# Two loads moved in the order of a DMA queue: attention with pooled queries and a two-branch maxout layer

## The chip, the cores and the metric

The kernel runs on one core of a Trainium2 chip. The metric is the device time of one execution in microseconds (us). The kernel before takes 358.24 us, the median of three runs (357.92 to 360.69). One further execution was profiled; every row of the profile comes from that one.

## The reference

```python
# attention: batch 8, heads 8, seq 1152, head_dim 64, float32
q_pool = q.reshape(B, H, S // 2, 2, D).mean(axis=3)        # (the pairs of neighbouring queries are averaged)
attn   = softmax(q_pool @ k.transpose(0, 1, 3, 2) / sqrt(D))
x      = (attn @ v) -> rows (batch, pooled position), columns (head, d): 4608 x 512
# maxout layer: d_model 512, d_ff 1024
out    = maximum(x @ w1, x @ w2) @ w_out                    # 4608 x 512
```

The kernel computes `maximum(h1, h2)` as `h2 + relu(h1 - h2)`: `wd = w1 - w2` gives the branch through the relu, and `w2 @ w_out` is multiplied once, ahead of time.

## The kernel before, in words

The work is cut into 32 pairs of heads (four pairs to a batch). In this text Q11, K11 and V11 are the loads of pair 11 and so on; each is 576 KB. A pair passes through these stages:

- SyncE (SP) issues the loads of Q (line 358), K (346) and V (370) into one of three buffers each, `qraw`, `kraw`, `vraw`. In DRAM a Q load has 128 rows of 4.6 KB, a K or V load has rows of 2.3 KB.
- GpSimd (POOL) adds the neighbouring queries (`cast_q`, line 435, to `qp`), and converts K (`cast_k`, line 405, to `kbf`) and V (`cast_v`, line 445, to `vE`) to bf16. It also copies exponentials that are wanted later out of the way (`keep_rest`, line 468).
- K is transposed by a DMA that SP issues (`ktrans`, line 475, `kbf` to `kT`); Q is transposed by VectorE (DVE) in eight instructions (`qtrans_dve`, line 485, `qp` to `qpT`). The first five pairs take another way, through TensorE (PE).
- PE makes scores (line 302) in groups of 512 columns for two heads into PSUM banks `ps`; ScalarE (ACT) takes the exponential of each group (line 317) into `et`.
- PE multiplies the exponentials by V (lines 621 and 636), DVE divides by the sums (651, 654) into `xnat` and `xend`, and these are transposed to `xT`, mostly by a DMA of SP (lines 703, 712).
- The maxout layer runs in between: PE's h jobs (line 760), relu by DVE or ACT (771, 775), PE's p jobs (line 803), a copy to `stage` (809, 812), and two or more DMA stores from SP for each p job (lines 829, 835).

Nothing loops on the chip: all instructions are written out in the order of one long string, and one letter adds one operation to the program of one engine. `S` is a group of scores, `E` the exponential of the oldest group, `A` a piece of attention times V, digits are pieces of the maxout layer; `l` is the next load of a list of loads, `t` the next DMA transposition of K, `x` the next DMA transposition of the attention output, `o` the next store. Each engine runs its own operations in the order of the string and waits on semaphores for what they need. SP thus has one queue, and all its operations, a wait among them, hold up those behind:

```python
sp_line = {"l": [lambda a=a: {"q": load_q, "k": load_k, "v": load_v, "w": w_load}[a[0]](*a[1:])
                 for a in LOADS if a[-1] != "ACT"],
           "t": [lambda i=i: ktrans(i) for i in range(K_PE, NPAIR)],
           "x": [...],
           "o": [go for n in range(NP) for go in store_p(n)], ...}
```

A load also waits for ACT, so that loads do not run too far ahead. Where it stands in the string decides for which exponential: `done[0]` is the group of the last `E` ahead of it.

```python
def pace():
    g = done[0] - PACE                     # PACE = 2
    return [f"E{g}"] if PACE and g >= PACE_FROM else []
```

Of the kernel before, what the change touches and what calls it, by code (L numbers as in the profile page):

```python
# [116 lines left out]
def bass_funnel_attn__then__act_maxout2_kernel(  # L117
# [78 lines left out]
    with ctx:  # L196
# [728 lines left out]
        def step(c):  # L925
            if c == "S":
                m = int(next(banks))
                scores(group[0], m)
                exp_at.extend((group[0], go) for go in exps(group[0], m))
                group[0] += 1  # L930
            elif c == "E":
                g, go = exp_at.pop(0)
                go()
                done[0] = g
            elif c in lines or c in "0123":
                if c not in opened:
                    job = (moe if c in "0123" else lines[c]).pop(0)
                    opened[c] = job, int(next(banks)), list(job.units)
                job, m, units = opened[c]
                r, cost, mode, fence, go = units.pop(0)  # L940
                op("PE", lambda e: go(e, m), r=r, w=[f"b{m + n}" for n in range(job.width)], cost=cost,
                   mode=mode, fence=fence, tag=job.name)
                if not units:
                    del opened[c]
                    emptying.setdefault(c, []).extend((ev, job, m) for ev in job.evac)
            elif c in evacs:
                ev, job, m = emptying[evacs[c][0]].pop(0)
                eng, fn, cost = ev["eng"], ev["fn"], ev["cost"]
                if evacs[c][1]:
                    eng, (fn, cost) = "ACT", ev["alt"]  # L950
                op(eng, lambda e: fn(e, m), r=ev["r"] + [f"b{m + n}" for n in range(job.width)], w=ev["w"],
                   after=ev["after"], cost=cost, tag=("ev",) + job.name, alt=(ev["alt"] or (0, 0))[1])
            else:
                simple[c].pop(0)()
# [2 lines left out]
                 "m": ("Z", 0), "4": ("0", 0), "5": ("1", 0), "6": ("2", 0), "7": ("3", 0),  # L957
                 "8": ("0", 1), "9": ("1", 1), "+": ("2", 1), "-": ("3", 1)}
        for c in (
            "luFFlulllfyKQklgfbSkKEFlgFKSgESyFFlKEFgQSbESlFkSFEFFKlEySFSgESlqFFEFQlSbEFkSQElbKvSEgSlESceAAEATcESA"  # L960
            "EAhlkSaSEaASclEKAEglSAEcSAElvSaTaEhElTcSAESlAhAEScAElSSAcEAAlAqESa0a00aE0la0ScAE0SldQEaa00bSd0lEXSj0"
            "00ESvTl0h0E00eS4SlEAAkAEAlSa1ad1E1S1SEl1q1S1E1Kl1g1qE1S1SE1lQkrAEbArSdtAErArSE11avlEa1S5AElSdArESSrA"
            "dArEArSAEkAlaAaSEaAdatAESaXadjXEjSjSEXq0jl00jE0S0qr0E0lSr01rE11e41Sl1E1Sk1r10Er005St0ESv00r0ESSr0rvE"
            "lA4AAEASqalSaEAArAErAlSrSEEaAeaAArxAErSSaAEaAklrAAErS1at1ak1E1r0Sr0xE0r0Sr11E1rS1r0E050Sl0E0q0SrS0tE"
            "r01r10Er0eS0r0E0r0Skr0lE0r1S0r0E0rlSv0r1E14S11El1S1oSE1oAAEASAkEAaAlaSAEtAvSa1aE1SxS11ES111E1111ES11"
            "l1ESq5AAEAlSrSoEAroArAESrkSArEAaAalAEAaAaSvaaEtaSSrXEqArAjAEAjSrle00Ea0aS0rSE0lr0vSr0E1r01rlE114S11E"
            "1S1rSEA5AlvAEASr0E0ta0Eva0SrSE00xe00SE4AAkAESSlAEAaAaAEAlSa1aE1Sx000E0Sk11E0lS11E11S50qlE00tS00ESer0"
            "0rSE00rS0rE00r00Er0l0qSrSE0r01l1r0E14S11E1l1SroSE1r1o11roSErAoArAtEkArAAaaAArq1ESaa1E1Sx001r001E1r0S"
            "1rE0l001rS141E1rS1r1ES5AAEvAAroSSrvoESAlAAEvAaAaAlEAaAkaSa000SaEt0a000011114Ee111S111115E1S111Xl5EvS"
            "j00j0ESl0qSE0000SEl4AAAEArSSaEAaArAlqEArS1a1taE11rSESrE1e1xrS1r1EA5AAEASla0kaE0Sr00rSEq0l0r0SEr0ArAl"  # L970
            "E4SAAESr11aE1a1Srx1ESr11r1SEt5qAAAEArSe0aE0a0Slr0SEkr0S0r0E0lrS0r0E0r0Sl0rE0000ES0S0Er0tArAEArArS0aE"
            "0aq0Srx10Er1S14k1E1S11EroS1rSo1E1oAAoEvAAS1vElSAAlEAvAaSa1ESalAaAAEASa1aE1taS1rXvE1rS1j11Ej1eSrl11rE"
            "11qrSS5EAlAAkEAroS0a0oEa0S0rS0ErAAlAEASa0a0E0l0S4x00E0qSE0r00E0trSA4eAEAArS1a1Ea1k1Sr11ESr1lSr1E5AAA"
            "lEArS1a1Ea11Srx00E10S1l1E1S500tE0Sq0rS0Er00r0e0ESr00rSEl0kr00r0E0rS0l0ES00SE0A4AAEAAaAoaAoASaoSqaE11"
            "x11SESkr11t1rE11rE11rE1SrS1E1r11r1SEr11S1E1S11E1A5AEvAASoSvESlAAoAEvAaAaAElAaAa0Sa0a0E0taS00r0000E04"
            "e0Sx000r0E11141vS1x1E11r100500Sr11qE1Sr01lr110E1rS050E0Sl0r0E0SS0l0E0S0r0EArAArEAArlAkaAaArSE0etEa0a"
            "S0r0SE0rxS0rq0EA4AAEASkao1aE11o1SSE11lS11EA5AAElASa1aE1Sx0r00E0rS1rt0E0er0Sr0E1S4111ESl1r0q0E500S0lE"
            "0SrS0r0EA4lAAEAAAaaAASa1aESlk1Sx1r1ES1r11Ert11r11Er1qSSr1E1rArAEvAS1E11klS11El11vS1E1S1lvA5ESAAEAoAa"
            "oSaSESaAtaArAEArq00Ea0aSa00rExSv0r00ErS0xe0r0E0rSSr0kl0E0S00E0Sl00E0S00El0A4AEAAAaoSaSEoArAtArE00Ea0"
            "0aeS00rxE1111r00qS411E1111151S1k1E1r1Sl00500ESr000SrEl0A4AAEArSla1aE1S1S1EAAAEAlSa1aE1tSrS1rq1E1r1x1"  # L980
            "1rESSre11Er11rSk1Elr11S1E11Sl1E1A5AAEASaoSaEAoAAoEAoSa0a0tEq00rSESr0E00rx00k040E0AArvAArSrSvElArArAE"
            "AvaAaAAaAaSaSaE00a001x14E11S11E1x11Sv511E100S1SE0r1t11r0ES0500E0eSr00Er00SrSE0r00r0SEr0S00E0S00E0004"
            "0E00S0E0oS00oSE4AAAEAAaAaAeAAaEAaAAxAaAaAASa0aES0x00SE1000E0S411E1S11E111500S0E00S11E1S11E1S10E50S00"
            "E0S10E0Se10E00S00E0S00E0S00E10S41E11S11EoS11o1E1oSSo1E1AAEAAAaAaAAAaAaAxAAAAAaAaAAaAa1a1a1a11X1j11j1"
            "11111900001111111150000111o080110091o110000008101110191101000018111009101110000080101111191100000001"
            "001111910000000011111111110001000800110000o008001o11o00010181111Z9ZZZZZoZZoZZZZZZmZZZZzzZZZZZZZZZZmZ"
            "ZZZZZZzZzmzz"
        ):
            step(c)
# [52 lines left out]
```

## Time and profile before

| | |
|---|---|
| median of 3 runs | 358.24 us (357.92 to 360.69) |
| the profiled execution's own time | 358.12 us |
| its span, first to last instruction | 356.4 us |
| granted TensorE clock | 0.999 |
| PE busy | 346.0 us, 97% |
| ACT busy | 313.8 us, 88% |
| DVE busy | 230.1 us, 65% |
| POOL busy | 151.4 us, 42% |

Times within the profile count from the start of the span. PE is matrix multiplication, PEld the loading of its weights, which overlaps with it; both are issued in one stream. In a timeline row stand start, length, engine (a q means its sequencer: such rows are issues of DMAs, waits included), line, operation, names, shapes and how many instructions are merged; in square brackets the idle time before it and what ended it. "issue" there is idle time that nothing in the profile ended. A row of DMA issues ends with the size of one and the time from issue to landing.

### The profile page before, as it was taken

The numbers are of one execution on the slowest core, as the hardware profiler recorded it, in microseconds if no ns is written. First come the engines' busy times: TensorE is split into PE (matmuls) and PEld (weight loads), VectorE is DVE, ScalarE is ACT, GpSimd is POOL, SyncE is SP. The second block draws the span as 40 slices with busy tenths as digits, with TensorE's granted clock in tenths as the row PEclk, the third lists the DMA queues.
The fourth block names the chain that finished last, engine by engine and source line by source line (L and its number), as shares of the span: only waits on it lengthen the run. The fifth ranks groups of instructions, "written<-read, shape, count | busy, mean of one in ns | idle before, by whom it ended". The sixth has DMA issues, their size and how long they took to land.

```text
span 356.4 us, 13757 instructions
## 1 busy us (share of the span) xinstructions
PE 346.0 (97%) x6178; PEld 218.5 (61%) x6178; DVE 230.1 (65%) x472; ACT 313.8 (88%) x354; POOL 151.4 (42%) x136
## 2 busy tenths in 40 slices
PE   7889999999899999999999999999999999999996
PEld 5556665656564675656666576556576757448753
DVE  2587589974966867985887677785586875414001
ACT  5999999999999899999999989989999796992431
POOL 2625997554564264355544455227444621010000
PEclk9999999999999999999999999999999999999999
DMA  8999999999989989998999699998999943012215
GB/s 271 403 397 398 370 255 309 280 289 261 293 252 279 315 196 350 237 301 183 278 320 260 153 230 301 237 314 234 224 299 255 267 68 75 17 32 47 61 31 148
DMA packets 76699, 84.55 MB, mean 237 GB/s; under 512 B 48480, under 2 KB 49760, under 8 KB 76640
## 3 DMA queue, kind: packets, MB, share of 16 engines
q1 hardware_dynamic: 75856, 83.15, 87.5%
q8 instruction: 48, 0.79, 0.9%
q10 hardware_dynamic: 784, 0.52, 0.5%
q14 instruction: 11, 0.09, 0.1%
HBM read 62.91 MB, written 9.44 MB: 203 GB/s over the span
## 4 chain that ended last, share of the span: by engine, by line
PE 87%; ACT 9%; DMA 2%; issue 1%; SPq 0%; DVE 0%
PE ps L803 25%; PE ps L621 20%; PE ps L302 19%; PE ps L760 16%; ACT et L317 9%; PE ps L636 3%; PE ps L593 2%; DMA qraw<-in_q_dram 2%; PE ps L846 1%; PE ps L552 0%; PE ps L533 0%; SPq L346 0%; DVE qp L428 0%; SPq L358 0%; PE ps L730 0%
## 5 line engine op out<-in xcount | busy, mean ns | idle before, releaser
L317 ACT ACTIVATE et<-ps 128x1024 bf16<-128x1024 f32 (+1 forms) x336 | 302.4, 1019 | 14.5 <-PE ps L302 9.7
L302 PE MATMUL ps<-qpT,kT 64*128 64x256 bf16 (+7 forms) x1162 | 117.3, 283 | 2.7 <-issue 1.1
L485 DVE STREAM_TRANSPOSE qpT<-qp 32x288 bf16<-32x288 bf16 x216 | 101.4, 469 | 10.4 <-PE ps L302 6.1
L760 PE MATMUL ps<-xT,wd 64*128 64x512 bf16 (+3 forms) x832 | 81.2, 311 | 0.2
L302 PEld LDWEIGHTS ps<-qpT,kT 64*128 64x128 bf16 x1162 | 48.3, 94 | 49.7 <-ACT et L317 11.3
L803 PE MATMUL ps<-wo,stage 64*128 64x512 bf16 x544 | 76.4, 376 | 0.0
L435 POOL TENSOR_TENSOR qp<-qraw 128x576 bf16<-128x576 f32 x30 | 42.1, 1406 | 61.1 <-DMA qraw<-in_q_dram 57.3
L621 PEld LDWEIGHTS ps<-vE,et 128*128 128x128 bf16 x1728 | 54.9, 97 | 13.9 <-ACT et L317 9.3
L621 PE MATMUL ps<-vE,et 128*128 128x65 bf16 x1728 | 60.7, 193 | 0.7 <-issue 0.3
L771 DVE TENSOR_SCALAR stage<-ps 128x1024 bf16<-128x1024 f32 (+3 forms) x41 | 39.7, 970 | 21.1 <-PE ps L760 20.6
L760 PEld LDWEIGHTS ps<-xT,wd 64*128 64x128 bf16 x832 | 35.6, 94 | 22.2 <-PE ps L760 1.9
L405 POOL TENSOR_SCALAR kbf<-kraw 128x1152 bf16<-128x1152 f32 x31 | 35.7, 1153 | 26.3 <-DMA kraw<-in_k_dram 25.6
L803 PE MATMUL ps<-w,xT 64*128 64x512 bf16 x272 | 40.8, 377 | 0.0
L803 PEld LDWEIGHTS ps<-wo,stage 64*128 64x128 bf16 x544 | 26.4, 94 | 20.5
L445 POOL TENSOR_SCALAR vE<-vraw 128x1152 bf16<-128x1152 f32 x24 | 27.4, 1154 | 19.4 <-PE ps L636 10.8
L809 DVE COPY stage<-ps 128x1024 f32<-128x1024 f32 x14 | 17.1, 1224 | 23.1 <-PE ps L803 23.0
L468 POOL TENSOR_SCALAR stage<-et 128x1152 bf16<-128x1152 bf16 x14 | 16.1, 1152 | 35.5 <-ACT et L317 35.5
L654 DVE TENSOR_TENSOR xnat<-ps,rc 128x256 bf16<-128x256 f32 (+2 forms) x71 | 27.6, 397 | 2.0
L651 DVE RECIPROCAL rc<-ps 128x4 f32<-128x4 f32 (+2 forms) x64 | 11.6, 182 | 25.9 <-PE ps L621 25.5
L621 PEld LDWEIGHTS ps<-stage,et 128*128 128x128 bf16 x576 | 18.1, 97 | 2.7 <-issue 2.6
L621 PE MATMUL ps<-stage,et 128*128 128x65 bf16 x576 | 19.7, 193 | 0.0
L803 PEld LDWEIGHTS ps<-w,xT 64*128 64x128 bf16 x272 | 12.5, 94 | 8.8 <-DVE stage L771 0.2
(55 smaller groups left out, 155.4 us busy)
## 6 DMA issues: line engine op xcount, KB each, us to landing
vraw<-in_v_dram SPq DMA_DIRECT2D x32, 576.0 KB, 6.1
kraw<-in_k_dram SPq DMA_DIRECT2D x31, 576.0 KB, 6.7
qraw<-in_q_dram SPq DMA_DIRECT2D x31, 576.0 KB, 6.3
out_dram<-stage SPq DMA_DIRECT2D x24, 256.0 KB, 4.1
out_dram<-stage SPq DMA_DIRECT2D x21, 128.0 KB, 3.4
xT<-in_moe_w_dram SPq DMA_DIRECT2D x4, 512.0 KB, 12.2
stage<-in_moe_w_out_dram SPq DMA_DIRECT2D x4, 512.0 KB, 14.1
stage<-in_moe_w_dram SPq DMA_DIRECT2D x4, 512.0 KB, 13.2
```

What stands on the lines that cost most here:

```text
L302: last = e.matmul(ps[:, h, col:col + hi - lo], kT[i % 3][rows(h), t, :], qpT[i % 3][rows(h), lo:hi], start=True, stop=True)
L317: op("ACT", lambda e: e.activation(et2[:, :, c:c + z - a], ps[:, :, a - g * W:z - g * W], EXP, scale=scale), r=[f"b{m}", f"b{m + 1}"], w=w ...
L405: op("POOL", lambda g: g.tensor_scalar(kbf[s][:, :, :, :].rearrange("p t h d -> p h t d"), kraw[r][:, :, :, :], 1.0, 1.0, ALU.mult, ALU.mu ...
L435: op("POOL", lambda g: g.tensor_tensor(qpf[s][:, :, :], qraw[r][:, :, 0, :], qraw[r][:, :, 1, :], ALU.add), r=[f"qraw{r}"], w=[f"qp{s}.0", ...
L445: return g.tensor_scalar(vE[r][:, :, :, 0:D].rearrange("p t h d -> p h t d"), vraw[s][:, :, :, :], 1.0, 1.0, ALU.mult, ALU.mult)
L485: op("DVE", lambda e: e.transpose(view[dst:dst + 32, :, 32 * pb:32 * pb + 32], qpf[s][src:src + 32, :, 32 * db:32 * db + 32]), r=[f"qp{s}. ...
L621: last = e.matmul(fb[m][:, at * 66:at * 66 + 65], et[:, a:a + P], vE[vs][:, t, half, 0:65], start=(t == 0), stop=(t == NT - 1))
L654: todo.append(evac_op("DVE", lambda e, m, z=z, at=at, num=num, dst=dst: e.tensor_tensor(dst, a(m)[z, at:at + num, 0:D], rc[k][z, at:at + n ...
L760: last = e.matmul(fb[m + k][:, 0:size], wd[z, ct, (f0 + k) * P:(f0 + k + 1) * P], xT[z, ct, n0:n1], start=(turn == 0 and ct == 0), stop=(t ...
L771: return e.tensor_scalar_max(gT[:, f0:f0 + 2, g0:g0 + size], wide[m // 2][:, :, 0:size], 0.0)
L803: last = e.matmul(fb[m + k][:, :], lhs, rhs, start=(turn == 0 and j == 0), stop=(turn == 1 and j == NC_ + NF - 1))
L809: return e.tensor_copy(osb2[:, o:o + 2, :], wide[m // 2][:, :, :])
```

## The change

Two loads take a later place in SP's queue:

- The load of Q11 stood between the load of V8 and two stores of the output (both of one p job); it now comes behind these two stores, ahead of V9. By its place it waits for the exponential of group 85 instead of 84.
- The load of K29 stood between the load of Q29 and two stores, which are followed by the DMA transposition of K28 and one of the attention output; it now comes behind the two stores and the transposition of K28, ahead of the other transposition. By its place it waits for the exponential of group 260 instead of 258.

Nothing else in SP's order changes, the other loads wait for the same exponentials, and PE, ACT, DVE and POOL keep their orders. The string is otherwise written with other letters for the same thing: jobs of the maxout layer go by the digits 0 to 3 where they went by 0 and 1, and operations of different engines stand in another order to each other. The two places in the string (before, then after; the load is the `l` under the mark):

```diff
-            "l1ESq5AAEAlSrSoEAroArAESrkSArEAaAalAEAaAaSvaaEtaSSrXEqArAjAEAjSrle00Ea0aS0rSE0lr0vSr0E1r01rlE114S11E"
+            "333ES7AAEAkSroSEArolArAErSSrAElAavAaAEAaAaSaSaEStarXErAqAjAEljArS0ae0Ea0Sr0SElr0v0Sr0Elr10r1E114S11E"
# Q11:  before  ...AAEA l SrS o EAr o ArAE...        after  ...AkSr o SEAr o l ArAE...
-            "oSaSESaAtaArAEArq00Ea0aSa00rExSv0r00ErS0xe0r0E0rSSr0kl0E0S00E0Sl00E0S00El0A4AEAAAaoSaSEoArAtArE00Ea0"
+            "oSaSESaAtaqArAEAr22Eav2aSa22rExS2er22ErS2x2rk2E2rSSr2l2E2S22El2S22E2S22E2A6AEAAAaoSaSEoArAtlArE00Ea0"
# K29:  before  ...E l 0A4AEAAAa o SaSE o ArA t ArE...    after  ...A6AEAAAa o SaSE o ArA t l ArE...
```

More of the change, by code (lines that the diff above doesn't have):

```diff
@@ L959, in bass_funnel_attn__then__act_maxout2_kernel @@
         for c in (
[L960 to L964, printed above, removed]
@@ L965, in bass_funnel_attn__then__act_maxout2_kernel @@
-            "r01r10Er0eS0r0E0r0Skr0lE0r1S0r0E0rlSv0r1E14S11El1S1oSE1oAAEASAkEAaAlaSAEtAvSa1aE1SxS11ES111E1111ES11"
-            "l1ESq5AAEAlSrSoEAroArAESrkSArEAaAalAEAaAaSvaaEtaSSrXEqArAjAEAjSrle00Ea0aS0rSE0lr0vSr0E1r01rlE114S11E"
-            "1S1rSEA5AlvAEASr0E0ta0Eva0SrSE00xe00SE4AAkAESSlAEAaAaAEAlSa1aE1Sx000E0Sk11E0lS11E11S50qlE00tS00ESer0"
-            "0rSE00rS0rE00r00Er0l0qSrSE0r01l1r0E14S11E1l1SroSE1r1o11roSErAoArAtEkArAAaaAArq1ESaa1E1Sx001r001E1r0S"
-            "1rE0l001rS141E1rS1r1ES5AAEvAAroSSrvoESAlAAEvAaAaAlEAaAkaSa000SaEt0a000011114Ee111S111115E1S111Xl5EvS"
@@ L970, in bass_funnel_attn__then__act_maxout2_kernel @@
[L970 to L978, printed above, removed]
-            "oSaSESaAtaArAEArq00Ea0aSa00rExSv0r00ErS0xe0r0E0rSSr0kl0E0S00E0Sl00E0S00El0A4AEAAAaoSaSEoArAtArE00Ea0"
@@ L980, in bass_funnel_attn__then__act_maxout2_kernel @@
[L980 to L984, printed above, removed]
@@ L985, in bass_funnel_attn__then__act_maxout2_kernel @@
-            "11111900001111111150000111o080110091o110000008101110191101000018111009101110000080101111191100000001"
-            "001111910000000011111111110001000800110000o008001o11o00010181111Z9ZZZZZoZZoZZZZZZmZZZZzzZZZZZZZZZZmZ"
+            "lululllllyFFlflfKQglkblSkKlFEgFKlSgylESFFlKFEglQSblESlkFSlFEFFlKylSEFlSglESqlFFFElQSlbFEklSQEbKlvgES"
+            "SSElcAelAEATcESAhEAkSaSaEASlcEKAEgScAESAvESaaTEhETcSAESAhAEScAESScEqAEAaAaAaSa0E0c000dSAE0aSadQE0b0S"
+            "0vEXSj000EST0Eh0e00S4SEkAAAEAdSa1a1E1S1qSE11S1E1Kq1g1E1S1SkrE1QAEbdAtrSArEArvSlE1a1Ea1S5AdElSArESdSr"
@@ new lines, in bass_funnel_attn__then__act_maxout2_kernel @@
+            "AArEArkSAElAaAadtSEaAaAESadXajXEjSjSqElX2j22jE2qrS2r2El2Sr2e3El6333S3kE3rS3r30Evt070S0ESv0r00rESSr0E"
+            "l4qAAAElASaSaEArAArEArSSElaEAeaArAxAErSkSaaAElArAktArESa1a11Erx12rS2E2r2Sr11Er1Sr1q2El252S2E22rSSr2t"
+            "E23r32Er2eSr22Elr22Srk2E2r3Sr2v2Elr2Sr23E36S33El3S3oSE3oAkAEASAElAvaAaSAEtASa3aE3SxS33ES333E333q3ElS"
+            "333ES7AAEAkSroSEArolArAErSSrAElAavAaAEAaAaSaSaEStarXErAqAjAEljArS0ae0Ea0Sr0SElr0v0Sr0Elr10r1E114S11E"
+            "1Sr1vSEl5AAAEAvrS2aE2ta2E2erSSE22x2k2SE6AAAElSSAEAaAaAElASa3kaE3Sx000E0S33El0S3q3El33S70E0t0S00ErSe0"
@@ new lines, in bass_funnel_attn__then__act_maxout2_kernel @@
+            "r0SE0r0Sr0E0qr00r0El0r0SSrEl00r110E14S11El11SroSE1r1o11roSkErAoArAtEArAqAaaAAr1ESaa1E1Srx221r221E1r2"
+            "S1rEl22216S1r1E1Sr11ES5AAEvAAroSSrovESAlAEAlvAaAaAEAakAaSa333SaEt3a333300007Ee000S022224El2Sv222X6ES"
+            "j11qj1ElS1SE1111SEl5AAAEArSqSaElAaArAEArS3a3taE33rSESrE3e3xrS3r3EAk7AAElASa0aE0Sr00rSElq00r0SElr0ArA"
+            "E4SAAESr22aE2a2Srx2ESr22r2SEt6qAAAEArSe1aEl1a1Sr1SkEr1S1r1El1rS1r1El1r1S1rE1111ES1S1Er1tArAEArqArS1a"
+            "E1a1Srkx31Er3S353E3S33EroS3rSo3E3oAAoEvAAS3vElSAlAEAvAaSa3ElSaAaAAEASa3vaE3taS3rXE3reS3j33Elj3Srq33r"
@@ new lines, in bass_funnel_attn__then__act_maxout2_kernel @@
+            "E33rSS7kElAAAEAroS0a0oEa0S0rS0ElrAAAEASa0a0El0q2xS422E2SE2r2et2E2rSA6AEAAkrS1a1Ea11Sr11ElSr1Sr1El5AA"
+            "AEArS3a3Ea33Srx00E30S3l3E3qS700tE0S0rS0Er0e0r00ESr0k0rSEl0r00r0El0rS00ES00SE0A4AAEAAaAoqaAoASaoSaE22"
+            "kx22SESr22t2rE22rE22rE2SrS2E2r22r2SEr22S2E2S22E2A6AEvAASoSvESlAAoAEvAaAaAElAaAa1Sa1a1E1taS11r1133E35"
+            "e3Sx333r3E00070vS0x0E00r2114q11Sr22El2Sr12r221E2rS161El1S1r1El1SS11E1S1r1EArAkArEAArAaAeaArSElt1Ea1a"
+            "S1qr1xSE1rS1r1EkA5AAEASao3aE33o3SSEl33S33EA7AAElASa0aE0Sx2r22E2rS0rt2E2er2Sr2E0S6q000ElS0r11El411S1E"
@@ new lines, in bass_funnel_attn__then__act_maxout2_kernel @@
+            "1SrS1r1ElA5AAEAAAaaAkASa3aElS3xS3r3ES3r3t3Er3q3r33Er3SSr3E3rArAEvAS3E33klS33El33vS3El3S3vA7ESAAEAoAa"
+            "oSaSESaAtaqArAEAr22Eav2aSa22rExS2er22ErS2x2rk2E2rSSr2l2E2S22El2S22E2S22E2A6AEAAAaoSaSEoArAtlArE00Ea0"
+            "0aeS00rE1111rx00qS411E1133353S33El3r3S22722ESr222SrEl2A6AAElArSka0aE0S0S0EAAAElASa0aE0tSrS0r0Eq0r0x0"
+            "0rESSr0e0Er00rS0kElr00S0El00S0E0A4AAEASaoSaEAoAAoEAoSa1aq1tE11rSESr1E11rkx13353E3AArvArASrSvElArArAE"
+            "AvaAaAAaAaSaSaE33a332x27E22vS22E2x20S600E011S0SE1r0t00r1ES1411E1eSr11Er11SrSE1r11r1SEr1S11E1S11E1135"
@@ L987, in bass_funnel_attn__then__act_maxout2_kernel @@
+            "3E33S3E3oS33oSE7AAAEAAaAaAeAAaEAaAAxAaAaAASa2aES2x22SE0222E2S600E0S00E001433S3E33S11E1S11E1S13E53S33"
+            "E3S23E3Se23E33S33E3S33E3S33E23S72E22S22EoS22o2E2oSSo2E2AAEAAAaAaAAAaAaAxAAAAAaAaAAaAa2a2a2a22X2j22j2"
+            "20000+11110000333341111333o2923022-0o00222211+01000138331311123933322-0200022221+1010003383311111113"
+            "113332-21111111122222222221112100900220000o338332o22o333232-2222Z+ZZZZZoZZoZZZZZZmZZZZzzZZZZZZZZZZmZ"
             "ZZZZZZzZzmzz"
```

## The prediction

> **What bounds the kernel.** I read the page first, then the PE's timeline for the moments at which it stands still, then ACT, the queue of SyncE (SP) and the DMA packets around the two places of the change.
>
> ```profile
> span 356.4 us, 13757 instructions
> PE 346.0 (97%) x6178; PEld 218.5 (61%) x6178; DVE 230.1 (65%) x472; ACT 313.8 (88%) x354; POOL 151.4 (42%) x136
> q8 instruction: 48, 0.79, 0.9%
> PE 87%; ACT 9%; DMA 2%; issue 1%; SPq 0%; DVE 0%
> ```
>
> The chain that ended last is PE for 87% and PE is busy for 97%. A load that is issued at another moment can change the end only if PE or ACT waits less or more for it. The third line is a queue that carries instructions: 48 packets, 0.79 MB, so about 16 KB each. PE's 6178 matmuls and 6178 weight loads make 257 instructions per packet. I take this queue to be the refill of PE's instruction stream, in blocks of 256.
>
> PE has two gaps that no semaphore ends:
>
> ```profile
> 29.04 1.13 PE L621 MATMUL ps<-vE,et 128*128 128x65 bf16 x32 [0.35 <-issue]
> 92.70 0.61 PE L302 MATMUL ps<-qpT,kT 64*128 64x128 bf16 x8 [1.12 <-issue]
> 29.03:92.69 63.66, 61.99 (x1146) 38.46 (x1146) 47.31 (x101) 63.07 (x70) 43.83 (x38) 1.00 1.06 309
> 86.84:92.69 5.85, 4.73 (x140) 3.57 (x135) 5.38 (x14) 5.79 (x7) 3.29 (x4) 1.00 1.07 361
> ```
>
> The last two rows are sums over a stretch: its length, then busy time and count for PE, PEld, DVE, ACT and POOL, and at the end clock, DMA share and GB/s. Between the two gaps lie 1146 + 1146 = 2292 instructions, and 9 x 256 is 2304 (a few of PE's semaphore instructions are not in these counts). So both gaps stand at a seam between blocks: PE came to the end of a block and the next one was not there. The block before the second gap began at about 86.84 (140 + 135 instructions, with those that overlap the edges), and PE used it up in 4.73 us, because it holds many short 65-column matmuls. I take it that PE asks for the next block when it begins one, here at 86.84.
>
> Was the refill late? These are the DMA packets in four adjoining stretches (87.2 to 88.7, 88.7 to 90.25, 90.25 to 90.35, 90.35 to 91.5), and the instruction row of the third and of 26.5 to 26.6:
>
> ```profile
> DMA packets 265, 0.55 MB, mean 365 GB/s; under 512 B 29, under 2 KB 29, under 8 KB 265
> DMA packets 161, 0.63 MB, mean 406 GB/s; under 512 B 16, under 2 KB 16, under 8 KB 161
> DMA packets 31, 0.05 MB, mean 472 GB/s; under 512 B 15, under 2 KB 15, under 8 KB 30
> DMA packets 230, 0.44 MB, mean 381 GB/s; under 512 B 16, under 2 KB 16, under 8 KB 230
> q8 instruction: 1, 0.02, 68.5%
> q8 instruction: 1, 0.02, 69.3%
> ```
>
> Without the tiny packets the mean sizes are 0.55 MB / 236 = 2.3 KB (a V or K row of 9 x 64 floats), 0.63 / 145 = 4.3 KB (nearly all Q rows of 4.6 KB) and, after the refill, 0.44 / 214 = 2.05 KB (output rows of 2 KB). So the 16 engines did V8, then Q11, then PE's refill at 90.25 to 90.35, then the stores: the refill stood in line behind Q11. It took 68.5% x 16 x 0.1 = 1.10 us, so it ended near 91.4; PE went on at 92.70, 1.30 later. At the first gap the refill of 26.5 took 1.11 and PE went on 1.4 after its end. PE reached the seam at 92.70 - 1.12 = 91.58.
>
> The Trainium skill (page "Runtime: NRT & Kernel Launch", section "Instruction fetch mechanics") has the same 16 KiB blocks of 256 instructions, and calls the crossing mostly hidden. The trace agrees on the blocks; at 46 of the 48 refills it is hidden, and twice it costs 0.35 and 1.12 us.
>
> **The change, part one: Q11 behind two stores.** SP's queue around it (V8, Q11, two stores, V9), and the time from issue to landing of Q11 and of the stores:
>
> ```profile
> 84.72 0.58 SPq L370 DMA_DIRECT2D vraw<-in_v_dram  x1
> 86.13 0.34 SPq L358 DMA_DIRECT2D qraw<-in_q_dram  x1
> 87.48 1.27 SPq L829 DMA_DIRECT2D out_dram<-stage  x2
> 88.88 0.90 SPq L370 DMA_DIRECT2D vraw<-in_v_dram  x1
> qraw<-in_q_dram SPq DMA_DIRECT2D x1, 576.0 KB, 6.3
> out_dram<-stage SPq DMA_DIRECT2D x2, 256.0 KB, 4.9
> ```
>
> Now Q11 is issued at 86.13, ahead of the request of 86.84; the stores wait on SP for DVE's copy until 87.48. After the change Q11 is issued at 87.48 + 1.27 = 88.75, behind that request. By its place in the order string it also waits for the exponential one group later than before (85 for 84); groups take ACT under 1 us each, so at 88.75 that wait is long over. Nothing else on SP moves: V9 comes up behind Q11 at 89.1 (with Q11's 0.34), and now ends its issue, wait included, at 88.88 + 0.90 = 89.78.
>
> The refill then has V8 alone in front. Q11's own transfer is 576 KB at 406 GB/s = 1.45 us, so the refill starts at about 90.30 - 1.45 = 88.85, ends at 89.95, and PE could go on at 91.25, before it arrives at 91.58. The gap goes, with 0.33 us to spare. Bounds: the refill starts between 88.7 (V8's last packets) and 90.30 (no change), so the gap that is left is 0 to 1.12; I take 0.
>
> PE's 1.12 us is not all won. ACT's rows there, and the weight loads that wait for ACT next:
>
> ```profile
> 93.13 27.47 ACT L317 ACTIVATE et<-ps 128x1024 bf16<-128x1024 f32 x31 [0.49 <-PE ps L302]
> 97.07 0.76 PEld L760 LDWEIGHTS ps<-xT,wd 64*128 64x128 bf16 x10 [0.15 <-ACT et L317]
> 99.82 1.14 PEld L621 LDWEIGHTS ps<-vE,et 128*128 128x128 bf16 x36 [0.24 <-ACT et L317]
> ```
>
> ACT lost only 0.49 us to the gap: it was still at older exponentials. After it ACT runs 27.47 us with no idle time, and PE waits for ACT again from 97.07 on. PE would come there 1.12 earlier and wait longer; what moves the rest of the program is ACT's 0.49. Bounds 0.49 and 1.12; I take **0.5**, since the waits are within 5 us and the order is fixed.
>
> Late next are Q11 and its users; these are POOL's rows for Q11, a copy of exponentials and V9, and DVE's transpositions of Q11:
>
> ```profile
> 92.53 1.41 POOL L435 TENSOR_TENSOR qp<-qraw 128x576 bf16<-128x576 f32 x1 [1.80 <-DMA qraw<-in_q_dram]
> 93.90 1.16 POOL L468 TENSOR_SCALAR rem<-et 128x1152 bf16<-128x1152 bf16 x1
> 95.52 1.16 POOL L445 TENSOR_SCALAR vE<-vraw 128x1152 bf16<-128x1152 f32 x1 [0.46 <-DMA vraw<-in_v_dram]
> 95.31 2.38 DVE L485 STREAM_TRANSPOSE qpT<-qp 32x288 bf16<-32x288 bf16 x5
> ```
>
> The same bytes pass in another order. Q11 lands now at 86.13 + 6.3 = 92.4; behind the stores it lands between 93.0 (the second store, issued near 88.1, plus 4.9) and 93.8 (512 KB at 381 GB/s, 1.38 us, later); I take 93.4. POOL then adds the halves from 93.5 to 94.9, and DVE wants them at 95.31, or 94.8 after the gain. That hides it but for 0.1; with 93.8 DVE's five transpositions, and what is queued on DVE behind them, start 0.5 late, one for one. The copy of exponentials and V9 slip by 1.1 and 0.6, within POOL's idle time. The stores land up to 1.45 earlier, which nobody waits for here. Cost: 0, bounds 0 and 0.5.
>
> **Part two: K29 behind two stores and the transposition of K28.**
>
> ```profile
> 255.18 0.37 SPq L346 DMA_DIRECT2D kraw<-in_k_dram  x1
> 257.63 1.28 SPq L829 DMA_DIRECT2D out_dram<-stage  x2
> 259.01 2.53 SPq L475 DMA_TRANSPOSE kT<-kbf  x1
> 261.58 1.33 SPq L703 DMA_TRANSPOSE xT<-xnat  x1
> 262.96 0.57 SPq L370 DMA_DIRECT2D vraw<-in_v_dram  x1
> 268.77 1.68 SPq L475 DMA_TRANSPOSE kT<-kbf  x1
> kraw<-in_k_dram SPq DMA_DIRECT2D x1, 576.0 KB, 7.7
> kT<-kbf SPq DMA_TRANSPOSE x1, 6.3
> 262.96 1.15 POOL L405 TENSOR_SCALAR kbf<-kraw 128x1152 bf16<-128x1152 f32 x1 [0.89 <-DMA kraw<-in_k_dram]
> 270.35 1.40 POOL L435 TENSOR_TENSOR qp<-qraw 128x576 bf16<-128x576 f32 x1 [6.23 <-DMA qraw<-in_q_dram]
> ```
>
> K29 is issued at 259.01 + 2.53 = 261.55 instead of 255.18, 6.4 us later, and waits for exponential 260 instead of 258, which changes nothing by then. It lands behind K28's transposition, which lands now at 259.01 + 6.3 = 265.3: at the latest 265.3 + 1.45 = 266.8, at the earliest 1.45 sooner. POOL's conversion then ends by 268.0, and SP asks for it at 268.77 (transposition of K29). POOL's next work starts at 270.35. So K29 is hidden by 0.8 us; if it were later than that, the transposition and SP's queue behind it would slip one for one. The earlier landing of K28 wins nothing that a row shows as waited for. SP's next instruction, a transposition of the attention output, starts 0.4 later with K29's 0.37 ahead of it, and V29 behind that at 263.3 at the latest. The refill of PE that now has K29 ahead of it comes 1.45 sooner, but PE has no gap there to lose. Cost: 0, bounds 0 and the third rival's.
>
> **Sum.** 358.12 (the profiled execution: span 356.4 and 1.7 around it) - 0.5 = 357.6. That execution is 0.12 under the median of 358.24, so the forecast is **357.7**.
>
> **Rivals.** *The refill does not stand in line.* If PE's refill takes turns with SP's queue, Q11 does not hold it, the start at 90.30 is its own latency, and the gap stays: 358.2. For it: at most refills the gap does not come although loads are in flight. Against it: the packets lie exactly behind Q11 and ahead of the stores. The Trainium skill ("DMA: Bandwidth & Descriptors", section "Queues, rings and completion order") says just this, that each engine goes round its queues packet by packet; by that rule the time would be this rival's. The rows above speak for a line, so I give it 0.15.
>
> *The whole gap comes through.* PE keeps its 1.12 because ACT's run is itself short of work here and there: 358.24 - 1.12 = 357.1. Against it stand the waits for ACT from 97.07 on. 0.15.
>
> *Slower: a new gap at the seam near 271.* K29 now splits two transpositions and lies ahead of another refill. Rows: that refill (in the stretch 266.65 to 266.75), PE's count from the seam before it and PE at the seam after it, and the DMA share in 40 slices of 263 to 265:
>
> ```profile
> q8 instruction: 1, 0.02, 64.9%
> 263.92:271.13 7.21, 7.21 (x132) 4.63 (x128) 4.95 (x13) 7.21 (x9) 0.98 (x2) 1.00 1.06 360
> DMA  1214123922910114000089999999999999999999
> ```
>
> The refill ends at 266.70 + 64.9% x 16 x 0.1 = 267.74 and is usable at 269.04; PE is at the seam at about 271.1: 2.0 to spare. K29 ahead of it takes 1.45, and the next transposition, now alone, can add an idle stretch of its own like that of 263 to 264 (a share of a tenth or two): 1.0 to 2.0. Together 2.45 to 3.45, less what K28's transposition comes sooner (0 to 1.45). It decides from 2.0 on; the worst is a gap of 1.45, and if the first gap stays too, 359.7; with the first gain, 358.24 - 0.5 + 1.45 = 359.2. I give it 0.2 at **359.2**.
>
> **Chances.** Forecast 0.45, whole gap 0.15, no refill effect 0.15, new gap 0.2, something unseen 0.05, of either sign. The range runs from 357.1 less 0.3 (the spread of the two lower runs) = 356.8 to 359.7. One per cent, 3.6 us, is about what a measurement of this kernel can tell from no change, and no case above reaches it; only the unseen does. Faster by over 1% 0.03, within 0.91, slower 0.06.
>
> **What would show it.** Right: PE has no gap near 91 to 93 and the refill there starts by 89; ACT's idle time of 0.49 is gone; Q11's addition on POOL starts near 93.5; K29's conversion near 267; no gap at 270 to 272. Wrong: the gap near 91.6 remains with the stores ahead of the refill (no line), a gap marked issue appears near 271 (the slower rival), DVE idles before Q11's transpositions, or the transposition of K29 waits for POOL.

## The result, and the profile after

The changed kernel takes **360.01 us** (median of 22 runs, 358.53 to 363.11); the kernel before, run beside it on the same chip, 358.81 (22 runs, 356.96 to 360.69). The ratio of the runs compared is **1.0044, 95% interval 1.0029 to 1.0058**: 1.6 us slower, between 1.0 and 2.1. The forecast was 0.5 faster.

The page of the changed kernel, its span, busy times and chain, and two rows of PE's waits (total, times, longest):

```profile
span 358.0 us, 13756 instructions
PE 346.8 (97%) x6177; PEld 218.3 (61%) x6178; DVE 230.3 (64%) x472; ACT 313.8 (88%) x354; POOL 151.4 (42%) x136
PE 82%; ACT 12%; DMA 3%; DVE 1%; issue 1%; POOL 0%
PE ps L621 <- issue: 1.8, 2, 1.6
PE ps L302 <- DVE stage L771: 1.1, 1, 1.1
```

The span grew by 1.6. PE has the same instructions as before (one record is missing); its busy time is 0.8 longer, a rough figure since the ends of matmuls are modelled, and the rest is waiting. PE's timeline says where; these are the two gaps at seams that are left, the place of the old gap, and a gap at 99 that DVE ends:

```profile
28.32 1.22 PE L621 MATMUL ps<-vE,et 128*128 128x65 bf16 x35 [0.24 <-issue]
90.46 0.87 PE L302 MATMUL ps<-qpT,kT 64*128 64x64 bf16 x12
99.34 0.39 PE L302 MATMUL ps<-qpT,kT 64*128 64x64 bf16 x4 [1.13 <-DVE stage L771]
284.47 1.49 PE L621 MATMUL ps<-stage,et 128*128 128x65 bf16 x44 [1.56 <-issue]
```

The 1.12 us at 92.70 is gone: the scores at 90.46 run on, twelve in a row, where before the last eight stood and waited. In its place are 1.13 at 99.34 and 1.56 at 284.47, one behind each place of the change.

**Part one, the chain behind Q11.** SP's rows, the issue row of Q11 with its time to landing, and the packets in the stretches 87 to 88 (two rows), 88 to 89.5 (two rows), 89.5 to 90.2 and 90.2 to 91.2; the last row is of before, for the stores' stretch 90.35 to 91.5:

```profile
86.76 1.28 SPq L829 DMA_DIRECT2D out_dram<-stage  x2
88.09 1.46 SPq L358 DMA_DIRECT2D qraw<-in_q_dram  x1
89.61 0.44 SPq L370 DMA_DIRECT2D vraw<-in_v_dram  x1
qraw<-in_q_dram SPq DMA_DIRECT2D x1, 576.0 KB, 6.0
DMA packets 145, 0.31 MB, mean 311 GB/s; under 512 B 16, under 2 KB 16, under 8 KB 144
q8 instruction: 1, 0.02, 6.9%
DMA packets 146, 0.28 MB, mean 184 GB/s; under 512 B 11, under 2 KB 11, under 8 KB 146
q1 hardware_dynamic: 146, 0.28, 88.0%
DMA packets 121, 0.23 MB, mean 325 GB/s; under 512 B 10, under 2 KB 10, under 8 KB 121
DMA packets 54, 0.17 MB, mean 173 GB/s; under 512 B 11, under 2 KB 11, under 8 KB 54
q1 hardware_dynamic: 230, 0.44, 100.1%
```

The refill passes between 87 and 88, right behind V8, instead of at 90.25. But then the engines are slow. While SP waits for DVE's copy until 86.76, only V8 is under way, where before Q11 lay behind it; from 88 to 89.5 the engines move 184 GB/s (365 to 406 in the stretches before), and again 173 around the first packets of Q11. They do not stand idle for most of this: the packets of 88 to 89.5 filled 88.0% of the engines' time. Each packet took longer: 88.0% x 16 x 1.5 us / 146 = 0.145 us, where those of the stores before took 100.1% x 16 x 1.15 / 230 = 0.080. Why they do is open. Q11 lands at 88.09 + 6.0 = 94.1. To set executions beside each other I count from DVE's copy (line 809) that the stores wait for, at 85.51 here and 86.23 before: in the frame of before Q11 lands at 94.8, and there it was 92.4. It is **2.4 us later**. What that does, on POOL, DVE and ACT:

```profile
94.21 1.40 POOL L435 TENSOR_TENSOR qp<-qraw 128x576 bf16<-128x576 f32 x1 [4.51 <-DMA qraw<-in_q_dram]
95.65 2.40 DVE L485 STREAM_TRANSPOSE qpT<-qp 32x288 bf16<-32x288 bf16 x5 [1.50 <-POOL qp L435]
98.06 1.23 DVE L771 TENSOR_SCALAR stage<-ps 128x1024 bf16<-128x1024 f32 x1
99.77 1.02 ACT L317 ACTIVATE et<-ps 128x1024 bf16<-128x1024 f32 x1 [0.52 <-PE ps L302]
101.29 5.78 ACT L317 ACTIVATE et<-ps 128x256 bf16<-128x256 f32 x7 [0.49 <-PE ps L302]
```

DVE stands 1.50 before Q11's transpositions. Queued behind them is the relu of an h job at 98.06, which must empty two PSUM banks before PE can put its next scores there (99.34, 1.13 late); ACT then runs dry twice, for 0.52 and 0.49. The net of gain and loss is the time from the copy to the third relu (line 771), both released by PE; before, then after:

```profile
86.23 1.22 DVE L809 COPY stage<-ps 128x1024 f32<-128x1024 f32 x1 [3.58 <-PE ps L803]
103.62 1.22 DVE L771 TENSOR_SCALAR stage<-ps 128x1024 bf16<-128x1024 f32 x1 [1.04 <-PE ps L760]
85.51 1.23 DVE L809 COPY stage<-ps 128x1024 f32<-128x1024 f32 x1 [3.58 <-PE ps L803]
103.54 1.23 DVE L771 TENSOR_SCALAR stage<-ps 128x1024 bf16<-128x1024 f32 x1 [0.85 <-PE ps L760]
```

That is 17.39 before and 18.03 after: 0.64 longer. The copy itself comes 0.72 earlier in the changed kernel, with nothing changed ahead of it, so the two executions stand level again at the third relu. The 1.6 between the spans is therefore lost behind it.

**Part two, the chain behind K29.** K29, Q31 and K31 on SP; POOL's conversion of K29, its addition of Q31 and conversion of K31; and PE's refill in the stretch 281.6 to 281.8:

```profile
261.52 0.58 SPq L346 DMA_DIRECT2D kraw<-in_k_dram  x1
272.87 0.61 SPq L358 DMA_DIRECT2D qraw<-in_q_dram  x1
273.52 1.56 SPq L346 DMA_DIRECT2D kraw<-in_k_dram  x1
267.09 1.15 POOL L405 TENSOR_SCALAR kbf<-kraw 128x1152 bf16<-128x1152 f32 x1 [4.76 <-DMA kraw<-in_k_dram]
279.98 1.41 POOL L435 TENSOR_TENSOR qp<-qraw 128x576 bf16<-128x576 f32 x1 [4.40 <-DMA qraw<-in_q_dram]
281.56 1.15 POOL L405 TENSOR_SCALAR kbf<-kraw 128x1152 bf16<-128x1152 f32 x1 [0.17 <-DMA kraw<-in_k_dram]
q8 instruction: 1, 0.02, 38.8%
```

The same of before: Q31 and K31 on SP, on POOL, and the refill, here in the stretch 279.2 to 279.6:

```profile
271.80 0.57 SPq L358 DMA_DIRECT2D qraw<-in_q_dram  x1
272.57 0.37 SPq L346 DMA_DIRECT2D kraw<-in_k_dram  x1
277.75 1.40 POOL L435 TENSOR_TENSOR qp<-qraw 128x576 bf16<-128x576 f32 x1 [3.76 <-DVE rc L651]
279.33 1.15 POOL L405 TENSOR_SCALAR kbf<-kraw 128x1152 bf16<-128x1152 f32 x1 [0.19 <-DMA kraw<-in_k_dram]
q8 instruction: 1, 0.02, 16.5%
```

K29 itself is hidden, converted by 268.24, ahead of its transposition. But Q31 and K31 follow 1.1 and 1.0 later on SP and land some 2.2 later. PE began the block before this seam at 278.3 in both (256 instructions back from it); the refill started near 279.2 before and near 281.7 after, behind those loads. It took 38.8% x 16 x 0.2 = 1.24 us, so it ended near 282.9, and PE went on 1.5 later, at 284.47.

### The profile page after: what moved, and what is told of

The parts are those of the page before. It is cut to its first block, busy times and chain, and to the rows that moved or that the text cites. A ratio compares the mean times of both kernels' runs of the same rounds, so it can differ in the third digit from the quotient of the medians.

```text
span 358.0 us, 13756 instructions
## 1 busy us (share of the span) xinstructions
PE 346.8 (97%) x6177; PEld 218.3 (61%) x6178; DVE 230.3 (64%) x472; ACT 313.8 (88%) x354; POOL 151.4 (42%) x136
## 4 chain that ended last, share of the span: by engine, by line
PE 82%; ACT 12%; DMA 3%; DVE 1%; issue 1%; POOL 0%
PE ps L803 24%; PE ps L621 19%; PE ps L302 18%; PE ps L760 15%; ACT et L317 12%; PE ps L636 2%; PE ps L593 2%; DMA qraw<-in_q_dram 2%; PE ps L846 1%; DMA kraw<-in_k_dram 1%; DVE qpT L485 1%; PE ps L552 0%; POOL qp L435 0%; DVE stage L771 0%; PE ps L533 0%
```

## The experiments

**Theories.** For part one: the refill gain is real, but Q11 comes 2.4 late, and through DVE's fixed order (Q11's transpositions ahead of the relu) costs more than the gain. The rival: the gap at 99 is a matter of this one execution, or comes from part two. For part two, theory A: K29 between the two DMA transpositions slows the queue because it parts them. Theory B: the place among the transpositions does not matter; K29's transfer simply comes late, and what follows is pushed back. The rival to both: the gap at 283 comes and goes by chance.

Each kernel below but the changed one was run 12 times (before_fill12 10, before_fill20 13) with the kernel before beside it (358.63, 358.67 and 358.64 us in the three sets). Ratios are to that (that of after is from its own 22 runs); "copy to relu" is the time from line 809 to the third 771 as above; the gaps are PE's idle times, "issue" at 92 and 283, DVE at 99, with those under 0.13 us given as 0.

| kernel | ratio (95%) | copy to relu | gap at 92 | at 99 | at 283 |
|---|---|---|---|---|---|
| before | | 17.39 | 1.12 | 0 | 0 |
| before_again | 0.9979 (0.9950 to 1.0009) | 17.10 | 0.83 | 0 | 0 |
| k_only | 1.0006 (0.9978 to 1.0034) | 17.53 | 1.26 | 0 | 0.32 |
| k_stores | 1.0003 (0.9976 to 1.0031) | 17.08 | 0.80 | 0 | 0.83 |
| k_behind | 1.0024 (0.9999 to 1.0050) | 17.18 | 0.92 | 0 | 0 |
| after | 1.0044 (1.0029 to 1.0058) | 18.03 | 0 | 1.13 | 1.56 |
| after_again | 1.0048 (1.0017 to 1.0078) | 17.73 | 0 | 0.83 | 0.33 |
| q_only | 1.0010 (0.9980 to 1.0039) | 18.36 | 0 | 1.45 | 0.66 |
| q_dve | 1.0001 (0.9978 to 1.0025) | 16.67 | 0 | 0 | 0 |
| after_dve | 1.0021 (0.9998 to 1.0044) | 17.04 | 0 | 0.22 | 0.88 |
| v9_first | 1.0045 (1.0017 to 1.0072) | 18.05 | 1.10 | 0.44 | 0.23 |
| before_fill12 | 1.0081 (1.0051 to 1.0110) | 16.94 | 0 | 0 | 0 |
| before_fill20 | 1.0020 (0.9998 to 1.0041) | | | | |
| after_fill44 | 1.0035 (1.0012 to 1.0057) | 17.61 | 0.53 | 0 | 0.28 |

**q_only: part one alone.**

```diff
-  ESq5AAEA l SrSoEAroArAESrkS          (cut from the string, spaces set around the l)
+  ESq5AAEASrSoEAro l ArAESrkS
```

> Only Q11 goes behind the two stores; K29 stays. Theory (two costs): the PE gap near 91 to 93 is gone, but the DMA engines run half empty while the stores wait, Q11 lands over 1 us later than I forecast, DVE starts Q11's transpositions about 1.5 us late, and PE has a gap of about 1.1 us near 99 to 100 that DVE's copy at line 771 ends. Gain and loss nearly cancel: -0.5 to +0.6 us, no gap near 283. Rival (K29 is harmless, all of the loss of 1.6 us is Q11's): 1.6 us slower. Rival (my forecast; the gap near 99 is chance): 0.5 us faster, no gap near 99.

```profile
85.78 1.23 DVE L809 COPY stage<-ps 128x1024 f32<-128x1024 f32 x1 [3.58 <-PE ps L803]
104.14 1.22 DVE L771 TENSOR_SCALAR stage<-ps 128x1024 bf16<-128x1024 f32 x1 [0.85 <-PE ps L760]
99.93 0.39 PE L302 MATMUL ps<-qpT,kT 64*128 64x64 bf16 x4 [1.45 <-DVE stage L771]
284.15 1.49 PE L621 MATMUL ps<-stage,et 128*128 128x65 bf16 x44 [0.66 <-issue]
```

The gap at 99 is part one's own, with part two undone: 104.14 - 85.78 = 18.36. But there is a gap at 283 too, with K29 at its old place. That speaks for chance in part two. In time it is 359.36, a ratio that could be 0.7 us faster or 1.4 slower; the times alone do not settle part one, the profile does.

**q_dve: the same, with DVE's order changed.** Six of Q11's eight transpositions go behind relus that they stood ahead of. The cut gives DVE's order and not the string (r is a transposition, h a relu, three dots are other work):

```diff
-  r r r r r h4 r h5 r ... r h6
+  r r h4 r h5 r ... r r h6 ... r r
```

> Q11 behind the two stores, and six of its eight transpositions on DVE put behind the copies of the h jobs that they stood ahead of. Theory (Q11 costs only through DVE's order): no gap of PE near 91 to 93 and none near 99, and the gain of the forecast appears: 0.5 us faster than before, 0.5 to 1.1 faster than Q11 alone. Rival (what PE lost near 99 comes from another wait, such as the banks or the exponentials): the gap near 99 stays and the time is that of Q11 alone.

```profile
86.47 1.23 DVE L809 COPY stage<-ps 128x1024 f32<-128x1024 f32 x1 [3.58 <-PE ps L803]
103.14 1.23 DVE L771 TENSOR_SCALAR stage<-ps 128x1024 bf16<-128x1024 f32 x1 [0.54 <-PE ps L760]
```

Q11 is nearly as late as in q_only (its transpositions start 10.2 after the copy, there 10.5), but the relus no longer stand behind all of it: the gap at 99 is gone and the stretch is 16.67, shorter than before's. So the loss runs through DVE's order, and with that out of the way the refill's gain shows in this stretch. The time, 358.42, does not beat the kernel before: the 0.5 us that were expected lie inside its interval and are not shown by it.

**k_only, k_behind, k_stores: part two alone, in three places.** K29 as in the change; behind both transpositions; and ahead of both, behind the stores:

```diff
-  00E0S00E l 0A4AEAAAaoSaSEoArAtArE00Ea00aeS00rxE1111   before
+  00E0S00E0A4AEAAAaoSaSEoArAt l ArE00Ea00aeS00rxE1111   k_only
+  00E0S00E0A4AEAAAaoSaSEoArAtArE00Ea00aeS00rx l E1111   k_behind
+  00E0S00E0A4AEAAAaoSaSEo l ArAtArE00Ea00aeS00rxE1111   k_stores
```

> Only K29 goes behind the stores and the transposition of K28; Q11 stays. Theory: the loads behind K29 land 1.4 us later and more, the refill of PE's instructions that PE wants near 283 stands in line behind them, and PE has a gap marked issue of 1.0 to 1.7 us there; the gap near 92 is as before: 1.0 to 1.7 us slower. Rival (K29 hidden, the gap at 284 of the one profile is chance): same, within 0.3 us. Rival (V28's conversion on POOL is what is late): slower by 1 to 2 us, with PE's gap ended by POOL and not at a seam of 256 instructions.

> K29 goes one place further than in the change: behind the transposition of the attention output too, so the two transpositions stay together. Theory A (the split of two transpositions, each with its own idle stretch of the DMA engines, makes the later loads late): V29 lands no later than before plus 1.5 us, the loads behind lose under 1 us, no gap or a small one near 283: same to 0.5 us slower. Theory B (it is the time at which K29 is issued: the engines run dry before it, and its 1.45 us come on top later): the loads behind are late by 1.4 to 2.2 us as in the change, the gap near 283 is there: 1.0 to 1.7 us slower.

> K29 behind the two stores but ahead of the transposition of K28. Theory A (the split of the two transpositions makes the later loads late): nothing late behind it, V29 to K31 land within 0.5 us of before, no gap near 283: same. Theory B (the hour of the issue matters: the DMA engines are short of work before it): V29 and the loads behind it land 0.5 to 1.5 us later than before, with a gap of 0 to 1 us near 283.

The seam near 283 in k_only and in k_stores:

```profile
284.30 1.49 PE L621 MATMUL ps<-stage,et 128*128 128x65 bf16 x44 [0.32 <-issue]
282.93 1.49 PE L621 MATMUL ps<-stage,et 128*128 128x65 bf16 x44 [0.83 <-issue]
```

In all three the loads of Q30 and K30 land 1.0 to 1.5 later than before (counted from the stores at 257). In k_only and k_stores Q31 and K31 then land 1.7 to 2.1 late and the gap is there; in k_behind they are 1.2 to 1.6 late, the refill starts between 280.4 and 280.8, and it is not. K_stores does not part the transpositions and has the gap, so theory A is not needed. B fits these three better: wherever K29 stands, its transfer (1.45 us by the rate of the prediction) lies ahead of what follows. But it does not tell why 1.5 becomes 2 by Q31, and K29's place is not all of it: counted in the same way, K31 lands 1.2 to 1.6 late also in q_only, q_dve, v9_first and before_fill12, where K29 stands at its old place (0.2 in before_again). None of the three is slower beyond its interval, and k_only missed what was expected of it, a gap of 1.0 to 1.7 and as much in time.

**before_fill12, before_fill20, after_fill44: the seams moved.** `FILL` is the number of idle matmuls in the filler at the start of PE's program; 16 fewer or more move every seam by 32 instructions (16 matmuls and 16 weight loads) against the work.

```diff
-    FILL = 28
+    FILL = 12        # before_fill12; 20 in before_fill20; 44 in after_fill44
```

> The kernel before with 16 matmuls fewer in the idle filler that PE runs before the first data are there (FILL 28 to 12), so every seam between blocks of 256 instructions comes 32 instructions later in the program; no load, store or order changes. Theory (the gaps marked issue are late refills of PE's instructions, and a gap comes where a block is used up fast while loads stand in line): the block that PE used in 4.7 us before the gap at 92.7 now lasts over 6 us, so that gap goes; the one that ends near 283 shortens from 4.5 to 3.9 us, so a gap of 0 to 1 us appears there. Time within 0.6 us of before. Rival (the gap at 92.7 belongs to the instructions there, not to a seam): it stays at the same matmul.

> The kernel before with 8 matmuls fewer in the idle filler (FILL 28 to 20): seams 16 instructions later, so the block ahead of 92.7 lasts 5.8 us or more instead of 4.7 and the one ahead of 283 4.3 instead of 4.5. Theory: no gap near 92, at most 0.3 us near 283; 0.3 to 0.8 us faster than before, unless seams in the first 35 us get new gaps of up to 1 us. Rival: gaps do not follow the seams, time as before with the gap near 92.

> The changed kernel with 16 matmuls more in the idle filler (FILL 28 to 44): seams come 32 instructions earlier in the program. Theory: the block before the gap at 284 of the changed kernel lasts 5.0 instead of 4.5 us, so that gap is 0.5 us smaller or gone, while the wait of PE for DVE near 99 stays at 1 to 1.4 us. 0 to 1 us faster than the changed kernel. Rival (the gap at 284 is V28 coming late from POOL): it stays at the same matmul with 1.5 us.

Two rows of before_fill12 and one of after_fill44:

```profile
31.45 0.73 PE L621 MATMUL ps<-vE,et 128*128 128x65 bf16 x19 [1.12 <-issue]
94.48 0.29 PE L552 MATMUL ps<-ident,xnat 64*128 64x64 bf16 x8 [0.49 <-DVE xnat L654]
91.81 0.52 PE L621 MATMUL ps<-stage,et 128*128 128x65 bf16 x12 [0.53 <-issue]
```

With the seams moved and Q11 left where it was, the gap at 92 goes (copy to relu 16.94) and another, of 1.12, opens at 31.45, where no kernel with `FILL = 28` has one that long. In the changed kernel the moved seam brings 0.53 back at 91.81. All gaps of PE over 0.13 us marked issue between 22 and 290 us, in every profile, lie at the same place modulo 256 in PE's stream, the moved ones too: they are block seams. As kernels these are misses: before_fill12 is 2.9 us slower, of which the profile, of the fastest of its ten executions, shows 1.12 and 0.35 in new seam gaps; the rest is open. In after_fill44 the gap at 99 was expected to stay and is gone, and its time cannot be told from the changed kernel's. before_fill20 gains nothing. Its one profile is of an execution of 364.41 us, against a median of 359.79, and stays out of the sums below; it has a gap of 1.62 at 31.87 and, with both loads at their old places, one of 1.86 at the seam of 283, where 0.3 at most was expected.

**after_dve: both moves and the changed order of DVE.**

```diff
-  r r r r r h4 r h5 r ... r h6          (from the changed kernel)
+  r r h4 r h5 r ... r r h6 ... r r
```

> The changed kernel with both moves, and six of Q11's eight transpositions on DVE behind the copies of the h jobs. Theory (the first place costs through DVE): no gap of PE near 92 nor near 99, the stretch from the seam at 87 to the one at 100 is 1.2 to 1.6 us shorter than in the changed kernel; the late loads and a gap of 0.3 to 1.6 us near 283 stay. 0.7 to 1.6 us faster than the changed kernel, 0 to 1 us slower than before. Rival (the first place is worth nothing either way, all of the loss is at 283): time of the changed kernel.

The gap at 99 shrinks to 0.22 and the stretch to 17.04; the one at 283, which DVE's order cannot touch, stays at 0.88. The ratio falls from 1.0044 to 1.0021: about 0.8 us, with intervals that overlap.

**v9_first: V9 in Q11's old place, Q11 behind the stores.** This keeps the queue filled while SP waits for the copy.

```diff
-  ("v", 8), ("q", 11), ("v", 9),
+  ("v", 8), ("v", 9), ("q", 11),     # and Q11's l behind the two stores
```

> V9 takes Q11's place ahead of the two stores, and Q11 comes behind them; K29 as before. Theory (Q11's lateness in the change is order plus engines that are short of work while the stores wait): with V9 in the queue the engines stay at about 400 GB/s, so Q11 lands 1.2 to 1.8 us later than before instead of 2.4 to 2.7, and V9 ahead of PE's refill brings the gap near 92 back with 0.7 to 1.2 us. Rival (Q11 is late because a load behind stores is slow by itself): Q11 lands 2.4 us late or more, whatever stands ahead.

```profile
93.46 0.61 PE L302 MATMUL ps<-qpT,kT 64*128 64x128 bf16 x8 [1.10 <-issue]
95.73 1.41 POOL L435 TENSOR_TENSOR qp<-qraw 128x576 bf16<-128x576 f32 x1 [4.33 <-DMA qraw<-in_q_dram]
100.86 0.39 PE L302 MATMUL ps<-qpT,kT 64*128 64x64 bf16 x4 [0.44 <-DVE stage L771]
```

The half on the refill came as expected: with V9 in that place the refill is back behind a load, as it was with Q11, and the gap of 1.10 returns. The half on Q11 missed. Its addition starts at 95.73, with the copy at 87.01, so Q11 is still about 2.4 late; but here V9's 1.45 us stand ahead of it as well as the stores. What V9 does bring back is the speed of the packets: over both stores their 2 KB packets take 0.086 us on the mean, 0.084 to 0.095 in the kernels with Q11 in place, and 0.127 to 0.133 in those with nothing in that place. So the slow packets go with the empty place in the queue; how much of Q11's lateness they make, this run does not tell.

**before_again and after_again: both kernels once more, unchanged.**

> The kernel before once more, to see how far two profiles of one program differ. If the late loads and the gap near 283 belong to the change, there is no gap there again and PE's refill for that seam has over 1 us to spare; if they come by chance in any execution, there is a gap of some tenths of a us here too. The gap near 92 of about 1.1 us should be there again. Time: a ratio of 1.000 to before, within its interval.

> The changed kernel once more. If its two gaps belong to it: PE waits 1.0 to 1.5 us for DVE near 99, and has a gap marked issue of 0.3 to 1.6 us near 283; ratio to before 1.003 to 1.006. If one of them came by chance, it is missing here.

The kernel before repeats within its interval. The changed kernel repeats its loss (1.0048) and its gap at 99 (0.83, a little under what was expected), but the gap at 283 is 0.33 where it was 1.56.

## Why the prediction was wrong

**The step that failed** is the last of part one: "The same bytes pass in another order", and the cost that followed, "Cost: 0, bounds 0 and 0.5". Q11 was forecast to land 1.0 later (93.4 for 92.4), 1.4 at most; it landed 2.4 later. The bytes were the same, but they did not pass at the same rate: 184 GB/s for 1.5 us and 173 for 1.0, against 406, are 1.5 x (1 - 184/406) + 1.0 x (1 - 173/406) = 1.4 us of transfer not done, an estimate, and 1.0 + 1.4 is the 2.4. That the sum meets it so well is luck in part: 2.4 is the figure of one pair of executions. From the copy to Q11's addition on POOL it is 4.6 to 6.6 us in five profiles with Q11 in place (before, before_again, the three K kernels) and 8.4 to 9.3 in five with it moved (after, after_again, q_only, q_dve, after_dve), 3.1 apart on the means. The sign that was named for this came too: DVE idled 1.50 before Q11's transpositions. Nor did SP's queue stay as forecast: Q11's issue took 1.46 and not 0.34, and V9's ended 1.0 later.

The mechanism named there (DVE's transpositions "and what is queued on DVE behind them") is the one that came; its size was not. Over the profiles, the stretch is 18.04 with Q11 moved (mean of after, after_again, q_only), 17.26 with Q11 in place (before, before_again, the three K kernels) and 16.86 with Q11 moved and DVE's order changed (two). So the late Q11 costs 18.04 - 16.86 = 1.2 through DVE, and the refill gains 17.26 - 16.86 = 0.4; the forecast had 0 and 0.5. DVE's changed order was not tried with Q11 in place; before_fill12, with Q11 in place, the old order and no gap at 92, has 16.94, so the order by itself seems worth little.

**What was right in part one:** the refill stood in line. It started 2.1 to 2.6 us behind the copy with Q11 moved, and 3.8 to 4.3 behind it with Q11 or V9 in that place, and the gap at 92 went in all five profiles with Q11 moved and nothing in its place; only after_fill44, with its seams moved, kept half. The value of that gap, near ACT's 0.5 and not PE's 1.12, is what the stretch of 16.86 shows; the times are too wide to show it. The rivals "does not stand in line" and "the whole gap" fell.

**Part two: in the changed kernel's profile the mechanism was the slower rival's, its place was not.** K29 landed and was converted as forecast (267.1 for 267). The rival put a new gap at the seam near 271, where nothing came; it came near 283. I had looked at one refill behind K29 and not at the next ones, although everything behind K29 on SP was pushed back. The refill, if it was asked for at 278.3, started 3.4 us later, behind the loads, as at 90.25 behind Q11; both speak for standing in line. The Trainium skill ("DMA: Bandwidth & Descriptors", section "Queues, rings and completion order") has engines go round their queues packet by packet, where a packet is a batch of descriptors; how large a batch was here no run shows, so these rows do not decide against it.

**How much part two costs is open.** In the six profiles with K29 moved ahead of the second transposition the gap at 283 is 0.28 to 1.56, mean 0.70. In the seven others it is 0.13 on the mean, but two of these, both with Q11 moved, have 0.66 and 0.23. Sorted by both loads, the mean is 0 with neither moved (three profiles), 0.38 with K29 alone (three, k_behind among them), 0.30 with Q11 alone (three) and 0.76 with both (four): Q11's move goes with this gap nearly as much as K29's, with a scatter as large as the differences. The loads near 250 to 285 differ by 0.1 to 2.0 us between the two executions of the kernel before; why is not known. In time k_only, 1.0006, cannot be told from nothing. What is shown: both moves together lose 1.6 us (1.0 to 2.1), and again 1.7 (0.6 to 2.8). What the profiles suggest for the shares is 0.8 (18.04 - 17.26) for part one and about 0.6 (0.70 - 0.13) for the seam at 283, 1.4 of the 1.6; that the 0.6 is K29's is not shown.

The claim for the total, 357.7, thus failed by a term of 1.2 taken as 0 and a seam not looked at. That the loss lies within 1% of no change was right.

## What to carry to other kernels

Before a load is moved behind an instruction that waits, ask what the DMA engines have left to do during that wait: here the packets that came up behind the empty place passed at less than half the rate, and the load was late by more than what it was moved behind. Follow the late load through the engine with the fixed order, to the instruction queued behind its user, not only to its user. And when a transfer is pushed back late in a queue, look at every refill of PE's instructions behind it, not at the next one alone.

## What the runs showed of the hardware

- A block seam cost PE up to 1.56 us at 284.47. The seam is passed without a wait as long as the refill has been over for about 1.3 to 1.5 us (1.30 at 92.70 before, 1.5 at 284.47 after); no seam between 22 and 290 us in any profile was passed less than 1.2 us after the end of its refill.
- The Trainium skill ("Runtime: NRT & Kernel Launch", section "Instruction fetch mechanics") calls such crossings mostly hidden. Most were, here too; which ones were not depended on DMA loads elsewhere in the program and on 16 idle matmuls at its start.
- One load less in the queue during a wait of SP took the DMA engines from about 400 GB/s to 184, not by idling (their packets filled 88.0% of the time) but by packets of 2 KB that took 0.127 us on the mean where they took 0.086. With another load in that place they took 0.086 again.
